# Gated mix of linear and softmax attention: split weights kept in DRAM, sixty maxima units in the front, two-step cycles from step 159

## The chip, the cores and the metric

The kernel runs on one core of a Trainium2 chip. A core has five engines with a program of its own each: TensorE (PE, matrix products; PEld is its weight load), VectorE (DVE), ScalarE (ACT), GpSimd (POOL) and SyncE (SP, which here only issues DMAs). They wait for one another through semaphores. Operands lie in SBUF (128 partitions), results of matmuls in PSUM (eight banks of 128 x 512 floats). The metric is the time of one execution on the device in microseconds, less is better; compared are medians of runs.

## The reference: what is computed

```python
x = A_x                                                   # 2048 x 448, 16 heads of 28
g = sigmoid((x * gate_w).sum(-1, keepdims=True))
# A: linear attention
q, k, v = heads(x @ A_wqkv)
pq, pk = q @ w_phi, k @ w_phi                             # per head, 28 x 28
phi_q = concat(softmax(pq), softmax(-pq))                 # 56 features per head
phi_k = concat(softmax(pk), softmax(-pk))
kv, z = phi_k.T @ v, phi_k.sum(tokens)
a = ((phi_q @ kv) / (phi_q @ z + 1e-6)) @ A_wo
# B: softmax attention
q, k, v = heads(x @ B_wqkv)
b = (softmax(q @ k.T / sqrt(28)) @ v) @ B_wo
return g * a + (1 - g) * b
```

All of it is float32.

## The kernel before

**Precision.** TensorE is fed a rounded form of float32. Where full precision is needed, a number is split in a high part (rounded) and a low part (the rest), and a product is made of three passes: high by high, high by low, low by high. XH and XL are the parts of x, and a weight `w` has them as `w[:, 0]` and `w[:, 1]`. Splitting a weight (`split_weight`, lines 147 to 150) is a cast on ScalarE and a subtraction on VectorE. A matmul over the 448 rows of x has eleven passes (`x3`): four blocks of x with the high weight, four with the low one, three low blocks of x. `run` (line 115) issues passes in one go; `tok_major` (133) does it for a tile of 128 tokens and calls `mid(i)` ahead of each pass, so that other work can be put between passes.

**Order.** TensorE, VectorE, ScalarE and GpSimd run their instructions in the order of the program text. The DMA instructions on SP have an order that the scheduler chose; an instruction there that must wait holds up what stands behind it.

**Stages, in order of time.** (1) Up to about 62 us: loads, splits of x and the weights, first projections of B's q and k (`proj_qk`, `keep_qk`, which send the split result to DRAM). (2) The key stage to about 171 us, steps t = 0 to 15 of the loop at line 733: each step makes A's key tile `pk`, its features, the value tile `pva` (`value_a`), every second step adds two tiles to the key-value sums (`kv_add`), and on odd steps below 12 follows a projection of B. (3) The query stage, steps q = i - 16 of the same loop: the query tile `pq`, its features (`features1`: VectorE takes the largest and the smallest of each head, GpSimd subtracts one, and the engine given as `eng` the other; `features2`: sums, and GpSimd multiplies), the turned features (`turn`, tile `pft`), numerators (`numer`, tile `pn`), normalisation in four steps, and A's output projection `poa` with the weight woA_s (`out_a`). From q = 18 on each step also makes one tile of B's values `pvb` with wvB_s (`value_b`, tiles 0 to 7). (4) At about 313 us the loop ends. `stack` (842, 844) clears the buffers qst and kst, in which queries and keys are laid for the late loop (qst0, kst0 and kst1 by VectorE, the other four by GpSimd); `load_stack` fills them by DMA; value tiles 8 to 15 follow (loop at 956). (5) The late loop at line 1163, 256 steps: scores `st` (937), exponentials `p` on ScalarE (940), products with the values `pv` (1041). (6) Outputs of B, `pob`.

**Row maxima.** The softmax of B needs an upper bound per row that comes from row maxima of the scores, found ahead in 256 pieces of four matmuls each. A piece is either a *unit* of the front (`mx_unit`, 265 to 305) or a *visit* of the late loop (`mx_visit`, 311 to 357). A unit has four matmuls (line 291) into two PSUM tiles of two banks each, `pmb` and `pmd`; the keys are laid in pairs, one half of them as differences, so that ScalarE takes a Relu of `pmd` (294) and VectorE adds `pmb` and takes the maximum in two reduces (296). A visit has four single banks `pm` (328), one Relu (332), one such reduce (336) and two plain ones (339). `NF` is the number of units; 256 - NF visits remain. Keys and queries of units and visits come by DMA from DRAM (`pair_load`, `pair_query`, `mx_load`, `mx_query`).

Units are called from several places: at even key steps at the start and at the passes in `pace["at"]`, at q = 0, 1 and from 11 on, once after the stacks, and the `rest` of them spread over the 77 passes of value tiles 8 to 14.

**PSUM in the front.** `psn = [3, 2]`: three single banks `s` and two tiles of two banks `mx`, which `pmb` and `pmd` share (lines 74 to 77). After `psn[:] = 2, 3` there are two single banks, two tiles `mx` for `pmb` and one tile `md` for `pmd`, and the Relu result `rl` has two buffers instead of one.

**Steps of the late loop.** For s < `TWO` (191) each step scores 3 or 5 tiles by turns, multiplies the values of the step before and makes one visit. Behind `TWO` two steps go together: eight scores at an odd step, one visit at an even one, until the visits are done.

Of the kernel before, what the change touches and what calls it, by code (L numbers as in the profile page):

```python
# [8 lines left out]
F32 = mybir.dt.float32  # L9
# [17 lines left out]
SCALE = DH ** -0.5  # L27
EPS = 1e-6
NU = NG * NQ * 16
NF = 44  # L30
LOWEST = -3.0e38
OUTS = (200, 227, 206, 243)
PROJ = (218, 234, 248)
# [7 lines left out]
def gated_mix_kernel(ctx, tc, xT, wqkB, wvB, wvA, wkAT, wqAT, phi, woA, woB,  # L41
# [43 lines left out]
    ga_d = scratch("gad", [P, 4, D])  # L85

    o_d = dr.tile([(NG - 1) * GW, 2, S], F32, tag="od", name="od")

    ident = const.tile([P, P], F32, name="ident")
    make_identity(nc, ident)  # L90
# [101 lines left out]
    def mx_load(g, c):  # L192
        mxs[("kc", g, c)] = r = mx_tile("kc", f"kc{g}_{c}", 5)
        if c == 0:
            mxs["kd"] = mx_tile("kd", f"kd{g}", 1)
            for h in range(3):
                mx_rows(mxs["kd"], (h,), k_d[g], (h,), h * 512)
        for h in range(4):
            mx_rows(r, (h,), k_d[g], (h,), 512 * (c + (c == h and c < 3) - (c == h + 1 and c > 0)))
        if c < 3:  # L200
            js, t = slice(32 * c, 32 * c + DH), mxs["kd"]
            diffs.append((mxs["u"] + mxs["f"] // 4, lambda: nc.gpsimd.tensor_sub(  # L202
                r[js], f32(r[js]), f32(t[js]))))
# [9 lines left out]
    def pair_load(g, c):  # L213

        hp, b = divmod(c, 2)
        heads = (2 * hp, 2 * hp + 1)
        r = mx_tile("kc", f"kp{g}_{c}", 5)
        t = mx_tile("kd", f"kt{g}_{c}", 1)
        mx_rows(r, (0, 1), k_d[g], heads, b * 1024)
        mx_rows(r, (2, 3), k_d[g], heads, b * 1024 + 512)  # L220
        mx_rows(t, (2, 3), k_d[g], heads, b * 1024)
        mxs[("kp", g, c)] = r

        def sub():
            for i in (2, 3):
                js = slice(32 * i, 32 * i + DH)
                nc.gpsimd.tensor_sub(r[js], f32(r[js]), f32(t[js]))

        subs.append(sub)
# [35 lines left out]
    def mx_unit():  # L265

        u = mxs["u"]
        if u == NF:
            return
        mx_fin()  # L270
        take_diffs(2)
        mxs["u"] = u + 1
        gq, r = divmod(u, 16)
        g, qb = divmod(gq, NQ)
        if gq < GM:
            c, qt = divmod(r, 4)
            hp, b = divmod(c, 2)
            col = 64 * gq + 16 * b + 4 * qt + 2 * hp
            if r in (4, 9):
                pair_query(gq + 1, r // 9)  # L280
        else:
            c, qt = divmod(r, QM)
            hp, b = divmod(c, 2)
            col = 64 * gq + 4 * QM * b + 4 * qt + 2 * hp
            if r == 0:
                mx_query(gq)
        qc, kc = mxs[("qp", gq, hp)], mxs[("kp", g, c)]
        pb, pd = ps_mx(f"pmb{u}", False), ps_mx(f"pmd{u}", True)
        for j in range(4):
            js = slice(32 * j, 32 * j + DH)  # L290
            nc.tensor.matmul((pb if j < 2 else pd)[:, j % 2, :], qc[js, qt * P:(qt + 1) * P],  # L291
                             kc[js, :], start=True, stop=True, tile_position=(32 * j, 0))
        rl = rlp.tile([P, 2, 512], F32, tag="rl", name=f"rl{u}", bufs=2 if psn[1] == 3 else 1)
        nc.scalar.activation(rl, pd, AF.Relu)  # L294
        for i in range(2):
            nc.vector.tensor_tensor_reduce(rl[:, i, :], pb[:, i, :], rl[:, i, :], 1.0, LOWEST,  # L296
                                           ALU.add, ALU.max, part[:, col + i:col + i + 1])
        if gq < GM and qt == 3 and qb == NQ - 1:
            pair_load(g + 1, c)
        if gq == GM and qt == QM - 1:  # L300
            mx_load(g, c)
        if r == 15:
            mx_reduce(gq)

# [167 lines left out]
    def take_exps(left=0):  # L472
        while len(exps) > left:
            exps.pop(0)()
# [78 lines left out]
    def load_woA(b):  # L553
# [6 lines left out]
                                  woA[32 * (h % 4):32 * (h % 4) + 32, h // 4, :])  # L560
        return raw[:, :, :D]

    def out_a(t):
        tb, tl = divmod(t, 2)
        po_of[t] = po = ps_s(f"poa{t}")
        run(po[:, :D], [x for g in range(NG)
                        for x in out_passes(oTs[tb][g // 2], g % 2 * 256 + tl * P, woA_s[:, :, :, :D], g)])
# [102 lines left out]
    for n in range(4, NP):  # L670
# [33 lines left out]
        if n in (14, 19):  # L704
            take_subs()
    pair_load(0, 2)
    load_fold(wqAT, "q")
    wqA_s = weights(1, "wqA_s")

# [20 lines left out]
        pace["n"] += 1  # L730


    for i in range(2 * NT + 11):
        t, q = i, i - NT
        y = q - 1
        tb = y // 2
        take_acts()
        if t < NT and t % 2 == 0:
            mx_unit()
            passes = (55 if t < NT - 4 else 44) + (4 if t >= 4 else 0)  # L740
            pace["n"] = 4 if t >= 4 else 0
            pace["at"] = [passes // 3, 2 * passes // 3] if t in (4, 6, 8) else [passes // 2]
        if q in (0, 1):
            take_exps()

        if t % 2 == 0 and 0 <= t - 4 < NT:
            kv_add(t - 4)
            kv_add(t - 3)
        if q == 2:
            bk_s.close()  # L750
            ta_s = ExitStack()
            ta = ta_s.enter_context(tc.tile_pool(name="ta", bufs=1, reuse_waits="tile"))
            stg = ta_s.enter_context(tc.tile_pool(name="stg", bufs=2, reuse_waits="tile"))
            KV = ta.tile([P, 512], F32, name="KV")
            kvT = kv_copy()
            turn4.append("")
            woA_s = weights(3, "woA_s")
            wvB_s = weights(2, "wvB_s")
            take_exps()
        if t < NT:  # L760
            pk = ps_s(f"pk{t}")
            tok_major(pk, t, wkA_s, D, tick)
            fk[t] = features1(pk, f"k{t}", nc.gpsimd)
            take_exps(1)
        if 0 <= q < NT:
            pq = ps_s(f"pq{q}")
            tok_major(pq, q, wqA_s, D)
        if q == 0:
            fk[NT - 1] = features2(fk[NT - 1], f"k{NT - 1}")
        if q in (1, 2):  # L770
            fq[q - 1] = features2(fq[q - 1], f"q{q - 1}")
        if 0 <= q < NT:
            fq[q] = features1(pq, f"q{q}", nc.vector if 0 < q < 9 else nc.gpsimd)
        if 0 <= t - 1 < NT - 1:
            fk[t - 1] = features2(fk[t - 1], f"k{t - 1}")
        if q in (0, 1) or q >= 11:
            mx_unit()
        if y >= 9 and y % 2 and tb - 4 < 8:
            oTs[tb - 4] = normalize4(ta, num.pop(tb - 4), f"a{tb - 4}", 2)
        if y >= 4 and y % 2 == 0 and tb - 2 < 8:  # L780
            numer(tb - 2)
        if q > 0:
            take_exps(int(q < NT))
        if q == 3:
            kv_out(kvT)
        if 2 <= q - 1 < NT:
            fq[q - 1] = features2(fq[q - 1], f"q{q - 1}")
        take_subs()
        if t == 1:
            pair_load(0, 3)  # L790
        if y >= 8 and y % 2 == 0 and tb - 4 < 8:
            num[tb - 4] = normalize3(*num[tb - 4], 2)
        if t < NT:
            value_a(t)
            if t % 2 and t < NT - 4:
                proj_qk(NP + t // 2, ev)
        if q in (0, 1):
            proj_qk(NP + 6 + q, ev)
        take_lows()
        if 2 <= i < 6:  # L800
            fold(wqA_s, "q", i - 2)
        if q == 1:
            ev_s.close()
        if q == 2:
            raws["woA"] = [load_woA(b) for b in (0, 2)]
        if q == 11:
            part_loads("wvB", wvB, D, "wvB")
        if q in (4, 6):
            split_part(woA_s, "woA", D, (q - 4) // 2)
        if q in (13, 15):  # L810
            split_part(wvB_s, "wvB", D, (q - 13) // 2)
        if q == 1:
            gates()
        if y < 9 or y % 2:
            if y >= 2 and y - 2 < NT:
                turn(y - 2)
        if 0 <= y - 10 < NT:
            out_a(y - 10)
            out_a2(y - 10)
        if y >= 9 and y % 2 == 0 and y - 2 < NT:  # L820
            turn(y - 2)
        if q == NT + 2:
            bd_s.close()
            vb = [value_tile(0)]
        if 0 <= q - NT - 2 < 8:
            value_b(q - NT - 2)
        if y >= 5 and y % 2 and tb - 2 < 8:
            num[tb - 2] = normalize2(ta, *num[tb - 2], f"a{tb - 2}", 2, True)
    ta_s.close()
# [34 lines left out]
        kst_of[(g, kb)] = load_stack(kst[(4 * g + kb) % 5], k_d[g], kb * 512, (0, 1, 0, 1))  # L864

    NS = NG * NQ * NT
    TWO = 191
    slots = {"n": 0}

    def p_slot(nm):  # L870
# [75 lines left out]
    stg = at  # L946
    load_q(0)
    load_nm(0)
    ps_s_.close()
    ps = ps_s_.enter_context(tc.tile_pool(name="psv", bufs=1, space=PSUM, reuse_waits="tile"))  # L950
    psn[:] = 2, 3
    turn4.clear()
    rlp = fr_s.enter_context(tc.tile_pool(name="rlp", bufs=1, reuse_waits="tile"))
    mx_unit()
    rest = NF - mxs["u"]
# [316 lines left out]
```

## Time and profile before

| | |
|---|---|
| median of 3 runs | 1009.05 us (1008.97 to 1009.34) |
| profiled execution | 1009.49 us, of which the span is 1007.7 |
| granted clock of TensorE, mean | 0.998 |
| DMA, mean | 98 GB/s, 98.89 MB |
| front unit, 44 times | ScalarE 45.2 us and VectorE 56.6 us in all |
| late visit, 212 times | ScalarE 132.2 us; VectorE 108.3 (first reduce, 159 times) and 304.8 (plain, 477 times) |
| scores, 1020 tiles | TensorE 303.4 us, ScalarE 529.3 us |

The profile is of one execution. Busy time of an engine does not count instructions that only wait or issue DMAs. A group of instructions is named by its line, engine, operation and tiles, with the count behind x; then come busy microseconds, mean nanoseconds, and the idle time before them with what ended it. The chain of waits is followed back from the last instruction: at each step to what released it, or to its predecessor on the engine; a piece has a start, a length and the work in it. A timeline row has start, length, engine, line, operation, tiles, and in square brackets the idle time before and its releaser. Since matmuls are pipelined, the lengths of neighbouring matmul rows overlap, and prices are better read from starts or from the chain.

### The profile page before, as it was taken

The numbers are of one execution on the slowest core, as the hardware profiler recorded it, in microseconds if no ns is written. First come the engines' busy times: TensorE is split into PE (matmuls) and PEld (weight loads), VectorE is DVE, ScalarE is ACT, GpSimd is POOL, SyncE is SP. The second block draws the span as 40 slices with busy tenths as digits, with TensorE's granted clock in tenths as the row PEclk, the third lists the DMA queues.
The fourth block names the chain that finished last, engine by engine and source line by source line (L and its number), as shares of the span: only waits on it lengthen the run. The fifth ranks groups of instructions, "written<-read, shape, count | busy, mean of one in ns | idle before, by whom it ended". The sixth has DMA issues, their size and how long they took to land.

```text
span 1007.7 us, 17959 instructions
## 1 busy us (share of the span) xinstructions
PE 998.3 (99%) x6472; PEld 556.3 (55%) x6472; DVE 677.6 (67%) x1338; ACT 803.5 (80%) x1532; POOL 241.8 (24%) x217
## 2 busy tenths in 40 slices
PE   9999999989999999999999999999999999999998
PEld 7878888868788433333333333333333344455656
DVE  6456666987636678888888888788887874544202
ACT  5445545667744899999999999999999999979682
POOL 1265456688526102110011110101201011101010
PEclk9999999999999999999999999999999999999999
DMA  8973100122335803333532223531324345515131
GB/s 297 316 242 96 56 33 25 49 82 82 92 107 136 168 7 87 83 76 76 120 66 75 47 64 89 105 85 50 89 53 98 79 98 144 148 37 148 63 105 55
DMA packets 64249, 98.89 MB, mean 98 GB/s; under 512 B 18176, under 2 KB 24944, under 8 KB 64160
## 3 DMA queue, kind: packets, MB, share of 16 engines
q1 hardware_dynamic: 64160, 97.74, 36.8%
q8 instruction: 51, 0.84, 0.4%
q14 instruction: 38, 0.31, 0.1%
HBM read 69.54 MB, written 27.78 MB: 97 GB/s over the span
## 4 chain that ended last, share of the span: by engine, by line
PE 95%; DVE 3%; POOL 1%; issue 0%; ACT 0%; DMA 0%; DVEq 0%; POOLq 0%; ACTq 0%
PE st L937 28%; PE pv L1041 25%; PE pm L328 9%; PE pqk L115 6%; PE poa L115 4%; PE pk L133 4%; PE pva L133 4%; PE pob L115 3%; PE pvb L133 2%; PE pq L115 2%; PE pvb L115 2%; PE pmb L291 2%; PE pqk L658 1%; PE pkv L485 1%; PE pft L531 1%; PE poL L1079 1%
## 5 line engine op out<-in xcount | busy, mean ns | idle before, releaser
L940 ACT ACTIVATE p<-st 128x512 f32<-128x512 f32 x1020 | 529.3, 639 | 25.8 <-PE st L937 25.8
L339 DVE TENSOR_REDUCE part<-pm 128x1 f32<-128x512 f32 x477 | 304.8, 686 | 135.1 <-PE pm L328 135.1
L937 PE MATMUL st<-qst,kst 128*128 128x512 f32 x1020 | 303.4, 424 | 0.3 <-DVE acc L1056 0.3
L1041 PE MATMUL pv<-p,vb 128*32 128x512 f32 x2048 | 266.1, 603 | 0.0
L937 PEld LDWEIGHTS st<-qst,kst 128*128 128x128 f32 x1020 | 168.0, 187 | 99.3 <-ACT p L940 48.6
L332 ACT ACTIVATE rl<-pm 128x512 f32<-128x512 f32 x212 | 132.2, 624 | 15.7 <-PE pm L328 13.9
L328 PEld LDWEIGHTS pm<-kc,qc 28*128 28x128 f32 x848 | 40.5, 181 | 177.8 <-issue 104.8
L426 POOL TENSOR_TENSOR oUb<-oUb,rsb 128x512 f32<-128x512 f32 x15 | 19.4, 1291 | 457.8 <-DMA rsb<-rdb 278.2
L336 DVE CUSTOM_DVE_ANT_0 rl<-pm,rl 128x512 f32<-128x512 f32 x159 | 108.3, 681 | 0.0
L328 PE MATMUL pm<-kc,qc 28*128 28x512 f32 x848 | 107.2, 495 | 0.0
L1041 PEld LDWEIGHTS pv<-p,vb 128*32 128x32 f32 x2048 | 45.4, 108 | 94.3 <-issue 87.6
L296 DVE CUSTOM_DVE_ANT_0 rl<-pmb,rl 128x512 f32<-128x512 f32 x88 | 56.6, 681 | 34.3 <-ACT rl L294 34.3
L115 PE MATMUL pqk<-XH,wB 128*128 128x512 f32 x192 | 59.3, 397 | 0.0
L294 ACT ACTIVATE rl<-pmd 128x1024 f32<-128x1024 f32 x44 | 45.2, 1028 | 7.9 <-PE pmd L291 4.3
L595 ACT CAST ev<-pqk 128x512 fp32r<-128x512 f32 x28 | 16.1, 589 | 38.7 <-PE pqk L115 31.3
L115 PE MATMUL poa<-woA_s,oTa 128*128 128x448 f32 x192 | 43.7, 375 | 0.6 <-POOL oTa L435 0.6
L115 PEld LDWEIGHTS pqk<-XH,wB 128*128 128x128 f32 x192 | 35.4, 188 | 8.5 <-issue 1.5
L1056 DVE SCALAR_TENSOR_TENSOR acc<-pob,gate,acc 128x448 f32<-128x448 f32 x12 | 8.2, 680 | 47.2 <-PE pob L115 47.2
L202 POOL TENSOR_TENSOR kc<-kc,kd 28x512 fp32r<-28x512 f32 x12 | 15.4, 1281 | 100.9 <-DMA kc<-qkd 43.9
L115 PEld LDWEIGHTS poa<-woA_s,oTa 128*128 128x128 f32 x192 | 34.7, 188 | 7.4 <-issue 3.8
L596 DVE TENSOR_TENSOR ev<-pqk,ev 128x512 fp32r<-128x512 f32 x28 | 19.0, 690 | 29.1 <-ACT ev L595 29.0
L115 PE MATMUL pq<-wqA_s,XH 128*128 128x448 f32 x128 | 38.5, 384 | 0.0
(163 smaller groups left out, 1179.5 us busy)
## 6 DMA issues: line engine op xcount, KB each, us to landing
qkd<-ev SPq DMA_DIRECT2D x28, 512.0 KB
qst<-qkd SPq DMA_DIRECT2D x64, 224.0 KB
kst<-qkd SPq DMA_DIRECT2D x64, 224.0 KB
od<-oTb SPq DMA_DIRECT2D x48, 112.0 KB
rsa<-rda SPq DMA_DIRECT2D x8, 512.0 KB
rsb<-rdb SPq DMA_DIRECT2D x15, 256.0 KB
kc<-qkd SPq DMA_DIRECT2D x64, 56.0 KB
gad<-ga SPq DMA_DIRECT2D x16, 224.0 KB
```

The lines of the kernel that those rows point to most:

```text
L115: nc.tensor.matmul(dst, l, r, start=i == 0, stop=i == len(todo) - 1)
L133: nc.tensor.matmul(dst[:, :n], l, r, start=i == 0, stop=i == len(todo) - 1, skip_group_check=True)
L291: nc.tensor.matmul((pb if j < 2 else pd)[:, j % 2, :], qc[js, qt * P:(qt + 1) * P], kc[js, :], start=True, stop=True, tile_position=(32 * ...
L294: nc.scalar.activation(rl, pd, AF.Relu)
L296: nc.vector.tensor_tensor_reduce(rl[:, i, :], pb[:, i, :], rl[:, i, :], 1.0, LOWEST, ALU.add, ALU.max, part[:, col + i:col + i + 1])
L328: nc.tensor.matmul(pm[j], mxs[("qc", gq)][js, qt * P:(qt + 1) * P], mxs[("kc", g, kb)][js, :], start=True, stop=True, tile_position=(32 * ...
L332: nc.scalar.activation(rl, pm[kb], AF.Relu if kb < 3 else AF.Copy)
L336: nc.vector.tensor_tensor_reduce(r, pm[j], r, 1.0, LOWEST, ALU.add, ALU.max, part[:, col + j:col + j + 1])
L339: nc.vector.tensor_reduce(part[:, col + j:col + j + 1], pm[j], AX.X, ALU.max)
L937: nc.tensor.matmul(st, kst_of[(gq // NQ, kt // 4)][:, j, (kt % 4) * P:(kt % 4 + 1) * P], qst_of[gq][:, j, :], start=True, stop=True)
L940: nc.scalar.activation(p, st, AF.Exp, scale=SCALE)
L1041: nc.tensor.matmul(pv[32 * j:32 * j + 32, :], vb[kt // 8][:, kt % 8, 4 * g + j, :], pt[j], start=kt == 0, stop=kt == NT - 1, tile_position ...
```

## The change

- `NF` goes from 44 to 60, so there are 196 visits. The three pairs of passes at t = 4, 6, 8 that have a second unit become six (t = 0, 2, 4, 6, 8, 10); value tiles 2 to 7 have one unit each at their sixth pass (q = 20 to 25); behind the stacks one unit comes at once and nine among the 77 passes, where there were one and two. With the last of the units `mx_load(g + 1, 0)` is called.
- woA and wvB are split in the key stage, two half-weights each, at t = 1, 3, 5, 7, with the subtraction in the next step; high and low parts are written to DRAM (`w_d`) and loaded into woA_s and wvB_s at q = 0. The splits at q = 4, 6, 13 and 15 go.
- The second subtraction of `features1` is VectorE's for 0 < q < 11, instead of 0 < q < 9, and GpSimd's else.
- The PSUM shape changes at q = 20 rather than after the stacks.
- `TWO` goes from 191 to 159.

```diff
@@ -27,7 +27,7 @@
 SCALE = DH ** -0.5
 EPS = 1e-6
 NU = NG * NQ * 16
-NF = 44
+NF = 60
 LOWEST = -3.0e38
 OUTS = (200, 227, 206, 243)
 PROJ = (218, 234, 248)
@@ -85,6 +85,8 @@
     ga_d = scratch("gad", [P, 4, D])
 
     o_d = dr.tile([(NG - 1) * GW, 2, S], F32, tag="od", name="od")
+
+    w_d = {nm: dr.tile([P, 2, 4, D], F32, tag=f"{nm}d", name=f"{nm}d") for nm in ("woA", "wvB")}
 
     ident = const.tile([P, P], F32, name="ident")
     make_identity(nc, ident)
@@ -299,6 +301,8 @@
             pair_load(g + 1, c)
         if gq == GM and qt == QM - 1:
             mx_load(g, c)
+            if c == NQ - 1 and qb == NQ - 1:
+                mx_load(g + 1, 0)
         if r == 15:
             mx_reduce(gq)
 
@@ -559,6 +563,32 @@
                 nc.sync.dma_start(raw[32 * c:32 * c + 32, i, :D],
                                   woA[32 * (h % 4):32 * (h % 4) + 32, h // 4, :])
         return raw[:, :, :D]
+
+    parts = [("woA", 0), ("woA", 2), ("wvB", 0), ("wvB", 2)]
+    part_raw = {}
+
+    def part_load(n):
+        if n < 4:
+            nm, b = parts[n]
+            part_raw[n] = load_woA(b) if nm == "woA" else load_part(wvB, D, nm, b)
+
+    def part_high(n):
+        nm, b = parts[n]
+        raw = part_raw[n]
+        high = stg.tile([P, 2, 512], F32, tag="stg", name=f"{nm}_high{b}")[:, :, :D]
+        nc.scalar.copy(high.bitcast(F32R), raw)
+        nc.sync.dma_start(w_d[nm][:, 0, b:b + 2, :], high)
+        part_load(n + 1)
+
+        def low():
+            nc.vector.tensor_sub(raw.bitcast(F32R), raw, high)
+            nc.sync.dma_start(w_d[nm][:, 1, b:b + 2, :], raw)
+
+        return low
+
+    def load_split(w, nm):
+        for i in range(2):
+            nc.sync.dma_start(f32(w[:, i, :, :D]), w_d[nm][:, i])
 
     def out_a(t):
         tb, tl = divmod(t, 2)
@@ -704,6 +734,7 @@
         if n in (14, 19):
             take_subs()
     pair_load(0, 2)
+    part_load(0)
     load_fold(wqAT, "q")
     wqA_s = weights(1, "wqA_s")
 
@@ -730,6 +761,7 @@
         pace["n"] += 1
 
 
+    part_low = []
     for i in range(2 * NT + 11):
         t, q = i, i - NT
         y = q - 1
@@ -739,9 +771,16 @@
             mx_unit()
             passes = (55 if t < NT - 4 else 44) + (4 if t >= 4 else 0)
             pace["n"] = 4 if t >= 4 else 0
-            pace["at"] = [passes // 3, 2 * passes // 3] if t in (4, 6, 8) else [passes // 2]
+            pace["at"] = [passes // 3, 2 * passes // 3] if t in (0, 2, 4, 6, 8, 10) else [passes // 2]
         if q in (0, 1):
             take_exps()
+        if part_low:
+            part_low.pop()()
+        if q == 0:
+            woA_s = weights(3, "woA_s")
+            wvB_s = weights(2, "wvB_s")
+            load_split(woA_s, "woA")
+            load_split(wvB_s, "wvB")
 
         if t % 2 == 0 and 0 <= t - 4 < NT:
             kv_add(t - 4)
@@ -750,12 +789,9 @@
             bk_s.close()
             ta_s = ExitStack()
             ta = ta_s.enter_context(tc.tile_pool(name="ta", bufs=1, reuse_waits="tile"))
-            stg = ta_s.enter_context(tc.tile_pool(name="stg", bufs=2, reuse_waits="tile"))
             KV = ta.tile([P, 512], F32, name="KV")
             kvT = kv_copy()
             turn4.append("")
-            woA_s = weights(3, "woA_s")
-            wvB_s = weights(2, "wvB_s")
             take_exps()
         if t < NT:
             pk = ps_s(f"pk{t}")
@@ -770,9 +806,15 @@
         if q in (1, 2):
             fq[q - 1] = features2(fq[q - 1], f"q{q - 1}")
         if 0 <= q < NT:
-            fq[q] = features1(pq, f"q{q}", nc.vector if 0 < q < 9 else nc.gpsimd)
+            fq[q] = features1(pq, f"q{q}", nc.vector if 0 < q < 11 else nc.gpsimd)
         if 0 <= t - 1 < NT - 1:
             fk[t - 1] = features2(fk[t - 1], f"k{t - 1}")
+        if q == NT + 4:
+            ps_s_.close()
+            ps = ps_s_.enter_context(tc.tile_pool(name="psv", bufs=1, space=PSUM, reuse_waits="tile"))
+            psn[:] = 2, 3
+            turn4.clear()
+            rlp = ta
         if q in (0, 1) or q >= 11:
             mx_unit()
         if y >= 9 and y % 2 and tb - 4 < 8:
@@ -794,6 +836,8 @@
             value_a(t)
             if t % 2 and t < NT - 4:
                 proj_qk(NP + t // 2, ev)
+                if t < 8:
+                    part_low.append(part_high(t // 2))
         if q in (0, 1):
             proj_qk(NP + 6 + q, ev)
         take_lows()
@@ -801,14 +845,6 @@
             fold(wqA_s, "q", i - 2)
         if q == 1:
             ev_s.close()
-        if q == 2:
-            raws["woA"] = [load_woA(b) for b in (0, 2)]
-        if q == 11:
-            part_loads("wvB", wvB, D, "wvB")
-        if q in (4, 6):
-            split_part(woA_s, "woA", D, (q - 4) // 2)
-        if q in (13, 15):
-            split_part(wvB_s, "wvB", D, (q - 13) // 2)
         if q == 1:
             gates()
         if y < 9 or y % 2:
@@ -823,7 +859,7 @@
             bd_s.close()
             vb = [value_tile(0)]
         if 0 <= q - NT - 2 < 8:
-            value_b(q - NT - 2)
+            value_b(q - NT - 2, (lambda i: i == 5 and mx_unit()) if q >= NT + 4 else None)
         if y >= 5 and y % 2 and tb - 2 < 8:
             num[tb - 2] = normalize2(ta, *num[tb - 2], f"a{tb - 2}", 2, True)
     ta_s.close()
@@ -864,7 +900,7 @@
         kst_of[(g, kb)] = load_stack(kst[(4 * g + kb) % 5], k_d[g], kb * 512, (0, 1, 0, 1))
 
     NS = NG * NQ * NT
-    TWO = 191
+    TWO = 159
     slots = {"n": 0}
 
     def p_slot(nm):
@@ -946,10 +982,6 @@
     stg = at
     load_q(0)
     load_nm(0)
-    ps_s_.close()
-    ps = ps_s_.enter_context(tc.tile_pool(name="psv", bufs=1, space=PSUM, reuse_waits="tile"))
-    psn[:] = 2, 3
-    turn4.clear()
     rlp = fr_s.enter_context(tc.tile_pool(name="rlp", bufs=1, reuse_waits="tile"))
     mx_unit()
     rest = NF - mxs["u"]
```

## The prediction

> **What bounds the kernel now.** The page first: busy times, then the chain that ended last.
>
> ```profile
> span 1007.7 us, 17959 instructions
> PE 998.3 (99%) x6472; PEld 556.3 (55%) x6472; DVE 677.6 (67%) x1338; ACT 803.5 (80%) x1532; POOL 241.8 (24%) x217
> PE 95%; DVE 3%; POOL 1%; issue 0%; ACT 0%; DMA 0%; DVEq 0%; POOLq 0%; ACTq 0%
> ```
>
> TensorE is busy for 99% of the span and holds 95% of the chain. So an edit is worth what it does to TensorE's own stream, and to the few gaps in it. Next come the busy times by stage (columns: window, its length, busy us and instructions of PE, PEld, DVE, ACT, POOL, granted clock, DMA share, GB/s).
>
> ```profile
> 184.00:214.00 30.00, 29.95 (x253) 25.30 (x252) 28.43 (x43) 21.68 (x37) 19.26 (x13) 1.00 0.17 52
> 214.00:224.00 10.00, 7.60 (x61) 5.38 (x59) 8.82 (x16) 6.51 (x11) 8.81 (x7) 0.83 0.31 87
> 361.49:805.86 444.37, 444.37 (x2755) 170.53 (x2753) 363.58 (x732) 430.51 (x860) 49.36 (x47) 1.00 0.34 76
> 824.20:860.21 36.01, 36.01 (x225) 16.23 (x225) 17.09 (x34) 35.78 (x73) 3.18 (x3) 1.00 0.51 134
> 957.05:964.87 7.82, 7.82 (x50) 3.89 (x49) 0.00 (x0) 7.82 (x18) 0.00 (x0) 1.00 0.83 210
> ```
>
> Three things are to be seen. One stage has an idle TensorE, the query stage near 214 to 224 us, and its clock is at 0.83 there. The late loop has no idle TensorE, with ScalarE nearly full beside it (430.51 of 444.37). And the price of two late steps depends on their form: the third window holds 86 pairs of one-step cycles (eight scores, two visits), 444.37/86 = 5.167 us each; the fourth 8 pairs of the two-step form with one visit, 36.01/8 = 4.50; the last 2 pairs without a visit, 7.82/2 = 3.91.
>
> **Late loop: two-step cycles from step 159.** Steps 159 to 190 are 16 pairs that go from the first form to the second, and the sixteen visits that they lose are the sixteen new units. The later visits shift within the same form: 158 + 38 = 196 visits end in the same step as 190 + 22 = 212 did. The gain is 16 x (5.167 - 4.50) = 10.7 us. Bounds: ScalarE's 35.78 us in those 8 pairs let the new form go no lower than 4.47 (gain 11.2), and the pair without a visit plus the dearest price of four maxima matmuls below, 3.91 + 0.63 = 4.54, gives 10.0. I take **-10.7**.
>
> **Sixteen units in the front.** TensorE's price comes from the chain of waits in the key stage (start, us, piece).
>
> ```profile
> 129.28 0.41 PE pva L133 x2
> 129.69 0.43 PE pmb L291 x2
> 130.12 0.01 PE pmd L291 x2
> 130.13 2.05 PE pva L133 x9
> ...
> 143.68 2.26 PE pva L133 x11
> ```
>
> A value tile without a unit takes 2.26 us; the one that a unit cuts in two takes 0.41 + 0.43 + 0.01 + 2.05 = 2.90. So a unit costs 0.63, more than its own 0.44. The bounds are 16 x 0.44 = 7.0 and 16 x 0.63 = 10.1; nearly all new units sit inside such tiles, so I take the dear end, **+10.1**. Moving maxima is by itself worth almost nothing: what the late loop gives, the front takes.
>
> ScalarE and VectorE also get this work (a Relu of 1.03 us and two reduces for each unit). Three units go to the key stage, six to passes of the value tiles before 313 us; there is room in both:
>
> ```profile
> L294 ACT ACTIVATE rl<-pmd 128x1024 f32<-128x1024 f32 x44 | 45.2, 1028 | 7.9 <-PE pmd L291 4.3
> ...
> 62.00:171.00 109.00, 109.00 (x931) 90.16 (x933) 69.49 (x152) 54.89 (x92) 57.86 (x50) 1.00 0.23 72
> 269.00:313.00 44.00, 44.00 (x253) 35.83 (x251) 14.47 (x37) 21.20 (x33) 11.77 (x11) 1.00 0.33 102
> ```
>
> **The weight splits.** In the query stage four subtractions on VectorE and four casts on ScalarE go. The groups by line and form (busy us, mean ns of one), what stands ahead of the stall on the chain, and the stall:
>
> ```profile
> L150 DVE TENSOR_TENSOR woA_s<-woA_raw,woA_s 128x896 fp32r<-128x896 f32 x2 | 3.7, 1855 | 0.2 <-issue 0.2
> L455 DVE TENSOR_TENSOR feat<-extq,pcq 128x448 f32<-128x448 f32 x8 | 8.1, 1014 | 0.8
> ...
> 209.01 2.62 DVE woA_s L150
> ...
> 214.62 0.57 ACT fT L534
> 215.19 1.70 POOL feat L467
> 216.89 0.90 POOL feat L453
> 217.79 1.54 POOL feat L455
> ...
> 216.94 1.32 PE L531 MATMUL pft<-ident,feat 128*128 128x128 f32 x8 [2.31 <-POOL feat L467]
> 217.92 1.09 PE L115 MATMUL pq<-wqA_s,XH 128*128 128x448 f32 x2
> ...
> 221.78 0.50 PE L291 MATMUL pmb<-kp,qp 28*128 28x512 f32 x2
> ...
> 227.68 2.23 PE pq L115 x11
> PE poa L115 <- POOL oTa L435: 0.6, 1, 0.6
> ```
>
> VectorE is busy for 28.43 of the 30 us before 214, and the 2.62 us subtraction stands in the chain that leads through GpSimd's feature operations to the one long gap of TensorE, 2.31 us. The query tile right behind the gap takes from 217.92 to 221.78, 3.86 us, where another takes 2.23: the granted clock was low, which costs 1.6. Half a microsecond goes later to a wait for GpSimd. All three together are 2.31 + 1.63 + 0.56 = 4.5. The 3.7 us of woA's subtractions come off just the engine that was full; from GpSimd it takes two feature operations over (queries 9 and 10), 2 x 1.01 us by the second row, which come behind the gap. I take **-4.5**; bounds 0 (the lateness is GpSimd's own) and -4.5. The rest of the stage is gapless.
>
> In the key stage the same eight operations come back, at the dearest mean above 8 x 1.86 = 15 us on the two engines together, in a window of 109 us with 40 and 54 us free. They can delay an operation that TensorE waits for by one subtraction's length at a time. I count +0.5, bounds 0 and 3 (one wait of the longest kind, 2.62). The DMAs of the halves (eight written, four read) are spread over a stage with a DMA share of 0.23: nothing, unless SP's queue is held up (a rival).
>
> **The banks at query step 20.** The switch from three two-bank tiles plus two single banks to two plus three comes before five more value tiles. The first tile to take the new shape waits for the copy of its predecessor (0.54 us, the ScalarE row below) and some issue time: **+0.2 to +0.75**, once; nothing else of the value stage had an idle TensorE.
>
> **The nine units behind the stacks.** This is where I expect the loss. Before, one unit comes right behind the clearing of the stacks and two among the 77 matmul passes of value tiles 8 to 14; after, one and nine, these behind 8, 17, 25, ... passes. The stacks' five VectorE memsets stand in program order between unit 49's reduces and unit 50's. Now the same place before (a value tile's copy on ScalarE, VectorE's order, TensorE's chain):
>
> ```profile
> 315.78 0.54 ACT L721 COPY vb<-pvb 128x448 f32<-128x448 f32 x1 [1.36 <-PE pvb L133]
> ...
> 313.34 1.76 DVE L842 MEMSET qst<- 128x2048 f32 x1 [0.66 <-PE pmd L291]
> ...
> 322.11 1.76 DVE L844 MEMSET kst<- 1x2048 f32 x1 [0.48 <-DVE kst L842]
> 323.80 0.62 DVE L296 CUSTOM_DVE_ANT_0 rl<-pmb,rl 128x512 f32<-128x512 f32 x1
> ...
> 324.97 0.07 DVE L296 DVE_READ_ACCUMULATOR2_ANT part<- 128x1 f32 x1
> ...
> 312.84 0.42 PE pmb L291
> 313.26 0.01 PE pmd L291 x2
> 313.27 7.90 PE pvb L133 x38
> 321.17 0.42 PE pmb L291 x2
> ```
>
> The memsets hold VectorE from 313.34 to 323.8, so the unit issued at 312.84 is reduced only by 325.04. Nobody minded: the next unit, at 321.17, had the second bank pair and the second Relu buffer. After the change the first unit behind the memsets takes one pair, the next (8 passes on) the other, and the third, at pass 17, needs the first pair again. TensorE gets there 17 x 7.90/38 + 0.44 = 3.97 us after 313.27, at 317.2; the pair comes free at 325.04. TensorE works in program order and everything behind, value passes too, waits: 7.8 us, or 7.6 with a unit at 0.63. I take **+7.7**. The stack DMAs, queued behind those units' tiles on SP, use that time, so they are not later than TensorE is. From there on units come every 8 to 9 passes (1.7 us or more, and 0.44 of their own), and VectorE needs 1.24 for each (323.80 to 325.04): no second stall.
>
> The clock after it: 2.31 us of idle time cost 1.63 above. I take **+2**, for a somewhat longer slow stretch after an idle time three times as long; bounds 0 and 3.3 (twice 1.63).
>
> [...]
>
> **Sum.** -10.7 + 10.1 - 4.5 + 7.7 + 2.0 + 0.5 (key stage) + 0.3 (banks) = +5.4. The profiled execution took 1009.49 us (span 1007.7 and 1.8 around it), 0.44 above the median of the runs, 1009.05. So 1014.9 in a profiled execution, **1014.4** by the median.
>
> **Rivals.**
>
> A: TensorE doesn't stand still behind the memsets (the third unit's pair is not the one that I think). Then the sum loses 9.7: 1004.7, and the change is a gain. For it: both other large terms cancel and the query gap is really gone. Against it: two bank pairs, two Relu buffers, one VectorE order. Chance 0.17.
>
> B: the query gap stays, because the chain behind 214 us is GpSimd's own (1.70, 0.90, 1.54 us in a row) and VectorE's new feature operations are late in turn; 1014.4 + 4.5 = 1018.9. Against it stands the 2.62 us row at the head of that chain. Chance 0.13.
>
> C: the late loop starts short of data. The two stretches before it, and the size of a stack load:
>
> ```profile
> 325.00:335.00 10.00, 10.00 (x54) 7.68 (x52) 2.57 (x10) 5.80 (x9) 5.39 (x4) 1.00 0.94 185
> 335.00:345.00 10.00, 10.00 (x68) 3.97 (x64) 6.96 (x14) 9.83 (x21) 0.00 (x0) 1.00 0.94 189
> ...
> kst<-qkd SPq DMA_DIRECT2D x64, 224.0 KB
> ```
>
> The DMA share is 0.94 up to the first scores, and stack loads now stand on SP behind key loads that wait for units 50 to 59. If they start later than TensorE's 7.7 us of standing cover, the first scores wait: 224 KB at 187 GB/s are 1.2 us, and a stack behind by three to seven such loads (3.6 to 8.4 us) gives 1018 to 1023. Chance 0.08.
>
> D: the same loss, with the cheap ends (units at 0.44, 3.1 us less; no clock loss): 1009 to 1011. Chance 0.07.
>
> **Chances and range.** My forecast 0.55 (its own range 1011.5 to 1017), A 0.17, B 0.13, C 0.08, D 0.07. A measurement here tells 0.2% from no change, 2 us. Faster holds A and a little of what lies between A and D: 0.19; same D and the low edge of my own: 0.10; slower 0.71. With A inside, the range is 1004.5 to 1019.
>
> **What would show it.** In the profile after: one gap of TensorE of 7 to 8 us at a matmul pmb, released by a VectorE reduce (L296's counterpart), behind the seventeenth pass from value tile 8 on, and a dip of the clock there; no gap of 2.3 us at pft; one-step pairs still 5.17 and two-step pairs 4.50; the key stage longer by three units and little else. I am wrong if TensorE has no gap behind the memsets, if the query gap stays, or if a new one appears in the key stage or at the first scores.

## The result and the profile after

The changed kernel takes 1020.12 us (median of 4 runs, 1018.32 to 1021.34), the kernel before 1009.09 (4 runs, 1008.97 to 1009.34): ratio 1.0108, 95% interval 1.0094 to 1.0122. It is slower by 11.0 us; 5.4 were forecast, and the time lies 1.1 us above the range. The profiled execution took 1020.6 us.

The page of the kernel after (its span) and TensorE's waits in its trace (us in total, times, the longest):

```profile
span 1018.8 us, 17970 instructions
...
PE pmb L293 <- DVE part L298: 7.5, 1, 7.5
PE pn L549 <- ACT fT L538: 3.1, 1, 3.1
PE st L973 <- DMA kst<-qkd: 2.9, 1, 2.9
...
PE pmb L293 <- ACT vb L752: 0.6, 1, 0.6
```

The first row of waits is the forecast gap, of the forecast size. The second stands where none was expected, and so does the third. Where the time went is read from windows by stage, before and after; first the key stage, the query stage and the value stage up to the first scores, of the kernel before, then of the kernel after:

```profile
62.76:171.68 108.92, 108.92 (x972) 90.36 (x970) 69.95 (x151) 54.81 (x93) 58.54 (x50) 1.00 0.23 70
171.68:268.85 97.17, 93.17 (x763) 75.40 (x756) 81.78 (x146) 70.32 (x116) 72.03 (x54) 0.98 0.23 71
268.85:331.00 62.15, 62.15 (x343) 51.53 (x341) 25.80 (x51) 27.82 (x43) 26.43 (x21) 1.00 0.47 123
```

```profile
62.37:173.14 110.77, 110.77 (x984) 90.69 (x982) 77.15 (x167) 60.32 (x100) 58.51 (x50) 1.00 0.37 117
173.14:268.15 95.01, 91.89 (x762) 75.50 (x755) 79.00 (x144) 66.93 (x112) 67.92 (x52) 0.98 0.28 95
268.15:348.75 80.60, 72.46 (x395) 54.24 (x394) 43.40 (x105) 41.27 (x57) 26.58 (x21) 0.96 0.38 98
759.02:830.87 71.85, 71.85 (x452) 32.27 (x449) 34.57 (x70) 71.42 (x145) 6.39 (x6) 1.00 0.36 86
830.87:840.02 9.15, 6.21 (x32) 2.53 (x28) 2.06 (x5) 4.72 (x10) 0.00 (x0) 0.81 0.57 111
```

The key stage is longer by 1.85 us (three units), the query stage shorter by 2.16, the value stage longer by 18.45. Sixteen pairs of steps from 159 on take 71.85 us, 4.49 each, where the one-step form takes 5.167: 10.8 gained. The next pair, steps 191 and 192, takes 9.15 instead of about 4.6: 4.5 lost, 2.94 of them an idle TensorE, the rest a clock of 0.81. Sum: 1.85 - 2.16 + 18.45 - 10.8 + 4.5 = 11.8, less 0.4 for an earlier start of the key stage and some 0.3 in other steps: the 11.1 by which the spans differ.

The gap in the value stage, on the chain of waits of the kernel after (start, us, piece):

```profile
316.54 0.42 PE pmb L293
...
317.03 1.76 DVE qst L878
...
325.80 1.76 DVE kst L880
327.57 0.55 DVE rl L298
...
328.79 0.79 PE pmb L293
...
329.58 3.28 PE pvb L135 x8
```

VectorE's memsets hold it from 317.03 until the reduces of the unit issued at 316.54 begin at 327.57, and only behind these can the third unit write its banks. Eight passes behind it take 3.28 us, where eight of 0.208 (7.90/38) take 1.66: the low clock (0.56 granted from 328.7 to 334 us) cost 1.6 there, and some 0.3 more before it was over.

### The profile page after: what moved, and what is told of

Same layout as the page of the kernel before. It is cut to its first block, busy times and chain, and to the rows that moved or that the text cites. A ratio compares the mean times of both kernels' runs of the same rounds, so it can differ in the third digit from the quotient of the medians.

```text
span 1018.8 us, 17970 instructions
## 1 busy us (share of the span) xinstructions
PE 999.2 (98%) x6472; PEld 560.6 (55%) x6472; DVE 666.7 (65%) x1340; ACT 810.3 (80%) x1532; POOL 237.8 (23%) x215
## 4 chain that ended last, share of the span: by engine, by line
PE 75%; DVE 1%; DMA 1%; issue 0%; ACT 0%; SPq 0%
PE st L973 28%; PE pv L1073 24%; PE pm L332 8%; PE poa L117 4%; PE pvb L135 3%; PE pob L117 3%; PE pmb L293 1%; DMA kst<-qkd 1%; PE pq L117 1%; PE pft L535 1%; PE poL L1111 1%; PE pn L549 1%; PE pvb L117 0%; DVE kst L878 0%; DVE kst L880 0%; PE poL L1181 0%
## 5 line engine op out<-in xcount | busy, mean ns | idle before, releaser
L343 DVE TENSOR_REDUCE part<-pm 128x1 f32<-128x512 f32 x441 | 281.7, 685 | 154.1 <-PE pm L332 153.9
L336 ACT ACTIVATE rl<-pm 128x512 f32<-128x512 f32 x196 | 121.7, 621 | 15.3 <-PE pm L332 14.1
L332 PEld LDWEIGHTS pm<-kc,qc 28*128 28x128 f32 x784 | 37.4, 181 | 164.3 <-issue 104.8
L298 DVE CUSTOM_DVE_ANT_0 rl<-pmb,rl 128x512 f32<-128x512 f32 x120 | 77.1, 680 | 43.1 <-ACT rl L296 42.9
L1073 PEld LDWEIGHTS pv<-p,vb 128*32 128x32 f32 x2048 | 48.1, 108 | 96.4 <-issue 89.7
L340 DVE CUSTOM_DVE_ANT_0 rl<-pm,rl 128x512 f32<-128x512 f32 x147 | 100.1, 681 | 0.0
L332 PE MATMUL pm<-kc,qc 28*128 28x512 f32 x784 | 99.2, 495 | 0.0
L296 ACT ACTIVATE rl<-pmd 128x1024 f32<-128x1024 f32 x60 | 61.7, 1028 | 26.4 <-PE pmd L293 23.2
L135 PE MATMUL pva<-wvA_s,XH 128*128 128x450 f32 x128 | 38.6, 375 | 0.0
L293 PE MATMUL pmb<-kp,qp 28*128 28x512 f32 x120 | 30.5, 503 | 8.1 <-DVE part L298 7.5
```

The source lines that it names most:

```text
L135: nc.tensor.matmul(dst[:, :n], l, r, start=i == 0, stop=i == len(todo) - 1, skip_group_check=True)
L332: nc.tensor.matmul(pm[j], mxs[("qc", gq)][js, qt * P:(qt + 1) * P], mxs[("kc", g, kb)][js, :], start=True, stop=True, tile_position=(32 * ...
L336: nc.scalar.activation(rl, pm[kb], AF.Relu if kb < 3 else AF.Copy)
L340: nc.vector.tensor_tensor_reduce(r, pm[j], r, 1.0, LOWEST, ALU.add, ALU.max, part[:, col + j:col + j + 1])
L343: nc.vector.tensor_reduce(part[:, col + j:col + j + 1], pm[j], AX.X, ALU.max)
L1073: nc.tensor.matmul(pv[32 * j:32 * j + 32, :], vb[kt // 8][:, kt % 8, 4 * g + j, :], pt[j], start=kt == 0, stop=kt == NT - 1, tile_position ...
```

## The experiments

All are compared with the kernel before, run beside them (medians 1009.7 to 1010.0); gains are counted from the changed kernel's 1020.12. That kernel was not run again beside them, and the kernel before is 0.6 to 0.9 us slower here than beside it, so a gain is uncertain by about as much.

**Two units in each of value tiles 2 to 7, three behind the stacks' first.**

```diff
-            value_b(q - NT - 2, (lambda i: i == 5 and mx_unit()) if q >= NT + 4 else None)
+            value_b(q - NT - 2, (lambda i: i in (3, 8) and mx_unit()) if q >= NT + 4 else None)
```

> The changed kernel, with two units in each of the value tiles 2 to 7 (at passes 3 and 8) and so only one and three behind the stacks. Theory (the gap of 7.5 us is the wait of the third unit for a bank pair that VectorE holds until the stacks are cleared, and the low clock behind it costs 2): the gap is gone, 1020.1 - 9.4 = 1010.7 us. Rival (the stacks' DMAs or the first scores are next in line and take the time): a new gap between 315 and 350 us and a gain of less than 4 us, 1016 or more.

1010.52 us (10 runs, 1008.44 to 1013.08), ratio 1.0009 (0.9998 to 1.0020): 9.6 gained. The wait that is left, the value stage, and pieces of the chain from one step of it (the three passes behind the second unit of a value tile, and the unit that comes next):

```profile
PE pmb L293 <- DVE part L298: 0.6, 1, 0.6
...
264.58:339.04 74.46, 73.07 (x395) 54.18 (x394) 43.23 (x105) 40.96 (x57) 26.54 (x21) 1.00 0.40 106
...
286.91 0.80 PE pvb L135 x3
...
287.75 0.50 PE pmb L293 x2
288.25 0.33 PE pmd L293 x2
```

The theory holds in kind: the gap and the slow stretch are gone (clock 1.00), and no wait at the first scores came in its place. That its figure of 9.4 was met is luck: the value stage itself fell only from 80.60 to 74.46, by 6.1. The edit took the rest back, since the unit of the next step now comes three passes behind the second one of this tile and its pmd is 0.33 us late, for a bank that ScalarE's Relu still reads. A step of this stage takes 1.06 us more for the added unit, not 0.63 (from one poa to the next 7.03 us, 274.51 to 281.54, against 5.97, 284.06 to 290.03, in the changed kernel); six times the difference of 0.43 are 2.6. The other 3.5 of the 9.6 come from the gaps at pn and at step 192, which differ from run to run: 1.3 and 1.9 us in this profiled execution (1008.56, next to the fastest of the ten), with a full clock behind both (1.000 in the mean of the execution, 0.993 in the changed kernel's), where the changed kernel's had 3.1 and 2.9.

**Three memsets instead of five on VectorE.** A dose of the suspected cause, with the units left where the change has them.

```diff
-        eng = nc.vector if nm in ("qst0", "kst0", "kst1") else nc.gpsimd
+        eng = nc.vector if nm in ("qst0", "kst0") else nc.gpsimd
```

> The changed kernel with kst1 cleared by GpSimd, so that VectorE has three memsets instead of five ahead of unit 50's reduces. Theory (TensorE's gap at the third unit lasts until VectorE has done its memsets): the gap falls by two memsets with their spacing, 2 x 2.2 = 4.4, from 7.5 to 3.1 us, and the time to 1020.1 - 4.4 = 1015.7. Rival (the gap has another end, ScalarE's Relu or the loads): the gap stays at 7.5 us, 1019 to 1021.

1012.65 us (10 runs, 1010.84 to 1015.39), ratio 1.0031 (1.0022 to 1.0041). TensorE's timeline of this kernel at the place:

```profile
326.32 0.50 PE L293 MATMUL pmb<-kp,qp 28*128 28x512 f32 x2 [3.13 <-DVE part L298]
...
326.76 0.70 PE L135 MATMUL pvb<-wvB_s,XH 128*128 128x448 f32 x2
```

The gap is 3.13 us, as worked out. The time fell by 7.5, not 4.4: behind this shorter gap the clock stayed full (0.50 and 0.70 us for rows that took 0.79 and 1.11 after the long gap), so the slow stretch of 1.9 us went as well. The value stage of this trace shows the two together, 74.27 us where it was 80.60 (270.14 to 344.41 us, clock 1.00). That is 6.3; the other 1.2 of the medians do not come from this stage. The profiled execution is the slowest of the ten, 1015.39, only 5.2 below the changed kernel's.

**Queries and maxima of block 12 loaded four steps sooner.** This is for step 192. SP's issues in the kernel after, and the chain there:

```profile
820.41 3.39 SPq L1134 DMA_DIRECT2D od<-oTb  x4
823.90 1.82 SPq L885 DMA_DIRECT2D kst<-qkd  x4
825.77 0.39 SPq L885 DMA_DIRECT2D qst<-qkd  x1
826.21 2.48 SPq L897 DMA_DIRECT2D qst<-nm  x4
829.58 4.21 SPq L885 DMA_DIRECT2D kst<-qkd  x4
```

```profile
829.58 5.50 DMA kst<-qkd
835.09 2.02 PE st L973 x4
```

The chain names a key load. But the key block that step 192 reads is another buffer, loaded long before; what it lacks is the last quarter of its queries and the maxima rows `qst<-nm`, issued behind four `od` stores, which wait for GpSimd (its last operation on oTb ends at 820.38), and behind four key loads. GpSimd had itself waited for a broadcast, `rsb`, which was issued at 810.11 and let it start at 817.04.

```diff
-            if kt == 12 and gq + 1 < NG * NQ:
+            if kt == (8 if gq == 11 else 12) and gq + 1 < NG * NQ:
                 load_q(gq + 1)
-            if kt == (12 if gq + 1 < 14 else 14) and gq + 1 < NG * NQ - 1:
+            if kt == (8 if gq == 11 else 12 if gq + 1 < 14 else 14) and gq + 1 < NG * NQ - 1:
```

> The changed kernel, with the queries and maxima of query block 12 loaded from step 184 on instead of 188, so that these DMAs stand ahead of the four od DMAs on SP. Theory (the wait at step 192 is for these queries and maxima, which stand behind od and behind key loads): the gap of 2.9 us near 835 is gone and the low clock behind it (1.6) too, 1020.1 - 4.5 = 1015.6. Rival (it is the key load, as the trace names it): unchanged, 1019 to 1021.

1016.38 us (5 runs, 1012.40 to 1017.23), ratio 1.0055 (1.0037 to 1.0074): 3.7 gained; the profiled execution is the slowest of the five, 1017.23. SP's issues and the chain of this kernel:

```profile
813.68 2.46 SPq L897 DMA_DIRECT2D qst<-nm  x4
822.81 3.43 SPq L1134 DMA_DIRECT2D od<-oTb  x4
826.34 3.57 SPq L885 DMA_DIRECT2D kst<-qkd  x8
```

```profile
832.15 2.27 PE st L973 x8
```

With the key loads as late as ever, the eight scores of steps 191 and 192 run through in 2.27 us. So the wait was for the queries and maxima, which the edit moves together, and the name in the chain was that of a neighbour on the same queue. In the trace of the kernel with three memsets the chain names the maxima (below).

**The row broadcast in four parts.** The gap at pn: ScalarE copies the turned features late, since in its order they stand behind the casts of the first normalised numerators, and these behind VectorE's multiplication with the broadcast rows rsa. Rows of the kernel after from VectorE, GpSimd, ScalarE and SP, then TensorE's behind the gap:

```profile
217.79 2.14 DVE L430 TENSOR_TENSOR oUa<-oUa,rsa 128x1024 f32<-128x1024 f32 x1 [0.79 <-DMA rsa<-rda]
...
217.14 1.71 POOL L471 TENSOR_TENSOR feat<-feat,fsumq 128x896 f32<-128x896 f32 x1 [0.73 <-DVE fsumq L470]
...
219.96 1.14 ACT L438 CAST oTa<-oUa 128x512 fp32r<-128x512 f32 x2 [3.58 <-DVE oUa L430]
...
221.86 1.05 ACT L538 COPY fT<-pft 128x512 f32<-128x512 f32 x2
...
209.32 0.54 SPq L424 DMA_DIRECT2D rsa<-rda  x1
...
222.47 1.16 PE L549 MATMUL pn<-fT,KV 56*32 56x256 f32 x32 [3.12 <-ACT fT L538]
223.56 4.26 PE L117 MATMUL poa<-woA_s,oTa 128*128 128x448 f32 x12
```

From issue to the multiplication are 8.5 us, for 512 KB. The twelve poa behind the gap take 1.4 us longer than in the kernel below (4.26 against 2.83): the clock was low again, 0.62 from 223.5 to 228 us.

```diff
-        nc.sync.dma_start(rs.rearrange("p n q -> p (n q)"),
-                          rd.unsqueeze(1).to_broadcast([4, 32, n * 512]))
+        if n == 2:
+            for j in range(4):
+                nc.sync.dma_start(rs[32 * j:32 * j + 32].rearrange("p n q -> p (n q)"),
+                                  rd[j:j + 1].to_broadcast([32, n * 512]))
+        else:
+            ...
```

> The changed kernel, with the row broadcast rsa (512 KB, read from DRAM) made as four DMAs of 32 partitions each instead of one of 4 x 32. Theory (the query stage now waits for the first normalisation, whose rsa took 8.4 us from issue to landing): rsa lands several us earlier, the multiplication on VectorE no longer waits, the gap of 3.1 us at pn and the slow stretch behind it (1.8) go, 1020.1 - 4.9 = 1015.2. Rival 1 (the broadcast is as slow in four parts): unchanged. Rival 2 (the casts' place in ScalarE's order is the cause, whatever the DMA does): the gap stays above 2 us or goes over to poa, 1018 or more.

1016.13 us (4 runs, 1014.77 to 1017.55), ratio 1.0062 (1.0046 to 1.0078): 4.0 gained. VectorE, GpSimd and TensorE of this kernel:

```profile
217.22 1.16 DVE L435 TENSOR_TENSOR oUa<-oUa,rsa 128x1024 f32<-128x1024 f32 x1
...
217.45 2.49 POOL L476 TENSOR_TENSOR feat<-feat,fsumq 128x896 f32<-128x896 f32 x1 [0.72 <-DVE fsumq L475]
...
222.01 2.83 PE L117 MATMUL poa<-woA_s,oTa 128*128 128x448 f32 x12
...
PE pn L554 <- ACT fT L543: 1.3, 1, 1.3
```

The multiplication no longer waits for its rows, the gap falls from 3.1 to 1.3 us and leaves the clock alone (granted clock 1.00 from 216 to 224 us). Only 0.8 of the 1.8 us is the wait for the rows. Another 1.0 is the multiplication's own length, 2.14 us in the kernel after and 1.16 here. There it came 0.65 us behind the start of a GpSimd multiplication and ended 1.08 us behind that one's end (218.85); here it came first, and GpSimd's took 2.49 us instead of 1.71. Rows that came a little late thus cost a place in turn besides: in the kernel with three memsets the rows were 0.40 us late, the multiplication took 2.53 us, and the gap was 3.1 us again. Both the theory and the second rival were partly right: 1.3 us are left, and they belong to the order of the engines.

**The three edits together.**

> The three edits together. Theory (three separate gaps): 1020.1 - 9.4 - 4.5 - 4.9 = 1001.3 us, below the kernel before by 7.8. Rival (they hide one another, or a next wait follows): 1005 or more.

1007.38 us (10 runs, 1006.60 to 1007.98), ratio 0.9974 (0.9965 to 0.9984). 12.7 gained where 18.8 were expected, so the rival's figure came true: 2.6 less by the crowded units, and the gap of 1.3 us at pn is still there. The three single gains (9.6, 3.7, 4.0) cannot be added either, since 3.5 of the first belong to the other two gaps. But it is below the kernel before, and the spread of its runs is 1.4 us instead of 3.

**The casts behind the copies.** The two lines that call `normalize4` go to the end of the step, behind `out_a`.

```diff
-        if y >= 9 and y % 2 and tb - 4 < 8:
-            oTs[tb - 4] = normalize4(ta, num.pop(tb - 4), f"a{tb - 4}", 2)
...
+        if y >= 9 and y % 2 and tb - 4 < 8:
+            oTs[tb - 4] = normalize4(ta, num.pop(tb - 4), f"a{tb - 4}", 2)
         if q == NT + 2:
```

> The three edits together, and the casts of the first normalised numerators (normalize4) put behind the features' exponential and the turned features' copies in ScalarE's order. Theory (the gap of 1.27 us that is left at pn comes from ScalarE standing at these casts, 1.73 us, with the features behind them): the gap is gone, 1007.4 - 1.3 = 1006.1 us. Rival (poa, which needs the casts, waits in its turn): a wait of 1 us or more at poa, 1007 to 1009.

1015.81 us (4 runs, 1014.53 to 1016.11), ratio 1.0061 (1.0046 to 1.0076). The theory falls, the rival is right and its price was set too low:

```profile
PE poa L117 <- POOL oTa L444: 5.5, 2, 3.6
```

The gap at pn is gone, and poa waits 3.6 and 1.9 us for GpSimd's low parts, which now stand behind its feature work. Behind the first of these waits the clock was low too (ten poa in 4.10 us, 2.33 behind the second).

**The multiplication ahead of the sums.** On the splits' part alone (next), the two lines that call `normalize3` go ahead of `features2`.

> The splits' part alone with rsa in four DMAs, and the multiplication of the numerators (normalize3) ahead of the features' sums in VectorE's order instead of behind them. Theory (the gap of 1.26 us left at pn is the 1.4 us that this multiplication stands behind the sums, though its rows have landed): the gap is gone, 1004.9 - 1.2 = 1003.7 us. Rival (the sums or poa are late in their turn): a wait of about the same size at another place, 1004.7 or more.

1005.87 us (5 runs, 1005.43 to 1009.01), ratio 0.9967 (0.9955 to 0.9980); no gain over the 1004.92 below. Again the wait moves: 0.7 us are left at pn, and poa waits 1.5 us for GpSimd's low parts.

**The splits' part alone, with the old broadcast and with four parts.** 44 units, the old passes and banks, TWO = 191; the edit is the diff above without its units, banks and cycles.

> The kernel before with the splits' part of the change alone: woA and wvB split in the key stage and kept in DRAM, two more feature subtractions on VectorE; 44 units, the old passes, banks and TWO = 191. Theory (the gap at pft goes, a gap of 1.3 to 3.4 us at pn comes, and the splits cost nothing in the key stage): 2 to 5 us below before, 1004.5 to 1007.5. Rival (the splits in the key stage and their DMAs cost as much as they bring): 1008.5 or more.

> The same with the row broadcast rsa in four DMAs. Theory: the gap at pn is 1.3 us with no low clock behind it, 5.4 us below before, 1003.7. Rival (the units and the two-step cycles are worth something by themselves): not below the 1007.4 of the three edits together.

1007.78 us (10 runs, 1005.18 to 1009.69), ratio 0.9978 (0.9966 to 0.9990), and 1004.92 us (4 runs, 1004.81 to 1005.18), ratio 0.9956 (0.9941 to 0.9971). The first lies just above its range, the second 1.2 above its figure and well below the rival's; it is the fastest kernel of this study. Its key and query stage:

```profile
63.12:171.97 108.85, 108.85 (x973) 90.37 (x971) 73.64 (x155) 57.78 (x97) 58.46 (x50) 1.00 0.38 120
171.97:263.71 91.74, 90.47 (x762) 74.02 (x755) 76.49 (x144) 66.92 (x112) 68.57 (x52) 1.00 0.33 103
```

The key stage takes 108.85 us against 108.92 before: the splits cost nothing there. The query stage takes 5.4 less. With the one-part broadcast the runs spread from 1005.2 to 1009.7, with four parts from 1004.8 to 1005.2.

**The kernel before with the broadcast in four parts.**

> The kernel before with the row broadcast rsa in four DMAs and nothing else. Theory (in the kernel before the splits on VectorE set the gap, the broadcast is hidden behind it): the gap of 2.3 us at pft stays, 1008.5 to 1009.7. Rival (the broadcast was the limit before as well, the splits were not): 2 us faster or more, 1007 or less.

1008.81 us (10 runs, 1008.29 to 1009.72), ratio 0.9993 (0.9983 to 1.0002): no change, as expected. Its trace keeps the old gap:

```profile
PE pft L536 <- POOL feat L472: 2.3, 1, 2.3
```

## Why the prediction came out right in direction and short in size

- **The memset gap** (+7.7, and +2 for the clock): 7.52 us, ended by unit 50's reduce, behind the seventeenth pass, with 1.9 for the clock. Shown by taking it away and by the dose. In the forecast this step carried the sign; in the runs the two failed terms below push the same way. No rival of the kind C (first scores short of data) came.
- **The units** (+10.1): the three in the key stage cost 1.85, 0.62 each. In the value stage 18.45 - 7.52 - 1.9 - 0.62 = 8.4 for 13 units, 0.65 each; 16 together +10.3.
- **The banks** (+0.3, bound 0.75): 0.62, once, behind ScalarE's copy, as described.
- **The key stage** (+0.5): nothing that can be seen.
- **The splits** (-4.5) is the first step that failed. That they caused the old gap was right: with the broadcast quickened it stays, without the splits it goes. (The run without them also hands two feature operations to VectorE, but GpSimd's first of these, at 217.79 in the prediction's lines, stands behind the gap.) That "the rest of the stage is gapless" behind it was wrong twice. First, the 2.3 us of delay covered the next arrival, the broadcast rows: from the stage's start to the unit ahead of pn 4.4 were gained (50.10 to 45.71 us), and up to the next unit 3.9 came back (8.06 to 12.00), by the 3.1 us gap and its 1.4 of low clock, less the poa wait that went. Second, the old stage had further waits near its end, for ScalarE's copies, among them these:

```profile
PE pmd L291 <- ACT fT L534: 0.8, 1, 0.8
...
PE pn L545 <- ACT fT L534: 0.3, 1, 0.3
```

They went with the change, and from the unit at 254.42 on (255.42 after) the stage is 1.7 shorter, 14.43 to 12.73, as it is with the splits' part alone. No term held that: the 2.2 gained in place of 4.5 are 4.4 - 3.9 + 1.7, the last by luck. Rival B put this place at no gain, by GpSimd's own chain; the cause was a late transfer and the order of the engines behind it. The 2.62 us subtraction that the prediction read as the head of the chain was long where a GpSimd multiplication, from 208.98 to 210.68, had begun just ahead of it (209.01); the other one began ahead of GpSimd's (200.61 against 200.83) and took 1.09.
- **The late loop** (-10.7, bounds 10.0 to 11.2) is the second. The price of a pair was right (4.49), 10.8 gained. But the sum held only TensorE's work: at step 192 the queries and maxima, paced by GpSimd's normalisation and by the queue, were late. SP's row of the od stores before:

```profile
810.02 3.40 SPq L1102 DMA_DIRECT2D od<-oTb  x4
```

From their issue to the first scores of the pair 191 and 192 there were 14.2 us (824.20 in the prediction's window), now there are 10.5 (820.41 to 830.87). That cost 4.5 in this profiled execution (the earlier loads won 3.7 by the medians), and no rival named it.

The forecast +5.4, corrected by 2.3 and 4.5, would have been +12.2; without the key stage's 0.5 and with the start 0.4 earlier it is 11.3, and 11.1 is what the spans show. The range reached to 1019.0 on the side where two of its terms failed together.

So the change's first part is a gain of 4 to 5 us once the broadcast is quick, and the units, banks and two-step cycles together are none, even without their two gaps: +10.3 + 0.6 - 10.8 by the stages above, and 1007.38 with them against 1004.92 without, about the 2.6 of the crowded units. No run has the sixteen units with neither the gap nor the crowding, so that last point is worked out and not shown.

## What to carry to other kernels

A gap that is removed can uncover the next arrival: ask for every other wait in that stage how early it was served before, in us, and not only whether it shows. A loop that is made shorter per step shortens the lead of every DMA that is issued so many steps ahead (here from 14.2 to 10.5 us), and a queue in order hands one late store's wait to the loads behind it (here od at 820.41 and the loads from 823.90 on). When work is spread over a stretch in which an engine is set to one long job, count the buffers between that job and TensorE.

## What the runs showed of the hardware

The 512 KB broadcast `rsa`, as one transfer of 4 x 32 rows, needed 8.5 us in the kernel after, from its issue to the multiplication that waited for it; in the profiles of this study the multiplication waited for it between not at all and 2.0 us, and with four parts the spread of the runs shrank (0.4 us in 4 runs against 4.5 in 10 with the splits alone; 3.6 in 5 with the multiplication ahead of the sums as well). The traffic in the 8.7 us from its issue on (busy tenths of 16 DMA engines, in 40 slices), in the kernel after, then over 9 us in the kernel with four parts:

```profile
DMA  1011004000223612402330312313223132233311
```

```profile
DMA  0021020378999498230000101000302102102069
```

As one transfer: mostly one to three tenths of the engines' time over the last 30 slices, 6.5 us. In four parts: seven to nine tenths in seven of the eight slices from 210.8 us on, 1.8 us. Why is not shown here.

The clock behind a gap of TensorE did not follow the gap's length alone in these traces. It was full behind 1.3 us (twelve poa in 2.83 us, with the broadcast in four parts), 1.9 (four scores in 1.15 us, with two units in each value tile) and 3.13 (granted clock 1.00 from 316 to 330 us, with three memsets). It was low behind 2.31 in the kernel before (0.66 from 216.94 to 222 us), behind 2.94, 3.12 and 7.52 in the kernel after (0.65 from 835.09 to 840.02, 0.62 from 223.5 to 228, 0.56 from 328.7 to 334), and behind 2.08. The row behind the gap of 2.08 us, in the kernel with three memsets, four scores in 1.95 us, where eight took 2.27 in the kernel with the earlier queries:

```profile
823.74 6.00 DMA qst<-nm
...
829.93 1.95 PE st L973 x4
```

Gaps of 3.12 and 3.13 us had opposite outcomes, and a low clock came behind 2.08 already. What else decides it is not shown here.

Maxima rows of 2 KB, issued behind key and query loads of 224 KB each, landed only 6.0 us after their issue (the row above), about as long as a key load issued behind them took in the kernel after (5.50 us).

Where VectorE's multiplication or subtraction of two SBUF tiles overlapped a GpSimd multiplication, in three places of these traces, the one that began second was longer by about what was left of the first: VectorE's 2.14 us (1.16 elsewhere) with 1.06 left, its 2.62 (1.09 elsewhere) with 1.67 left, GpSimd's 2.49 (1.71 elsewhere) with 0.93 left. Why is not shown here.
